# Sending x behind wq on the SP queue, and one V tile in two parts instead of four, in a decode kernel that streams its KV cache

## The chip, the core and the metric

One core of a Trainium2 chip runs the whole program. The metric is the device time in microseconds (us).

In the views, PE is TensorE (PEld its weight loads), DVE is VectorE, ACT is ScalarE, and SP is the engine that issues most transfers; a q behind a name means its sequencer. A semaphore is a counter that a transfer raises when its data have landed, and for which an engine can wait. A packet is the piece of a transfer that one of the 16 DMA engines moves at a time.

## The reference, cut to what matters

```python
# x [4,1,512], k_cache and v_cache [4,32,8192,128] bf16, wq [512,4096], wo [4096,512]; FFN width 1792
xn = layernorm(x)
q = (xn @ wq) per head
o = softmax(q . k_cache / sqrt(128)) @ v_cache
out = x + o @ wo + (silu(xn @ w_gate) * (xn @ w_up)) @ w_down
```

The K and V caches are 537 MB of the 551 MB that must be read. They come as 32 K tiles and 32 V tiles of 8 MB (4 heads each, 64 KB a partition).

## The kernel before: the parts concerned

Three 8 MB slots are used in turn. wq takes the first, and x, the layernorm's scratch and the q projection's scratch lie beside it; K0 and K1 take the other two. The first V tile can be loaded only when everything beside wq is finished.

```python
x_sb = beside_wq(B, D)                                   # 4 rows of 1 KB
nc.scalar.dma_start(out=x_sb, in_=x_flat[:, :])          # ACT's queue
nc.sync.dma_start(out=wq_t[:, 0:EC * H * Dh], in_=...)   # SP's queue, 4 MB
load_k(0); load_k(1)
# ... layernorm, transposition, q projection, zq ...
build_q(0); load_v(0)
for i in range(NT - 1):                                  # NT = 32
    turn_k(i, ...)                                       # VectorE transposes K_i
    if i >= 3:
        pv_to(i - 2, NK); load_k(i + 1)                  # K tile into the slot of V_(i-2)
    for g in range(NTG): score(i, g)                     # 64 matmuls
    ...
    elif i == NT - 2: load_v(i, (T // 4,) * 4)           # V30 in 4 transfers, T = 256
    else: load_v(i)                                      # one transfer of 8 MB
    # ... softmax of tile i, P.V of tile i-1 ...
# tail: wo, V31 in 7 parts of falling size, scores of K31, P.V of V30 and V31, wo, result
nc.sync.dma_start(out=out_flat[:, 0:DH], in_=res[0:B, :])
nc.scalar.dma_start(out=out_flat[:, DH:D], in_=res[QB:QB + B, :])
```

## Time and profile before

| | before |
|---|---|
| time, first three runs | 1286.03 us (1285.93 to 1286.06) |
| bytes, mean rate | 551.49 MB, 429 GB/s |
| DMA share, 0 to 1220 us / 1272 to 1279.4 us | 1.00 / 0.51 |
| last V part written | 1279.38 us |
| span in the profile | 1284.13 us |

The views that carry this (busy tenths, windows, end of the chain, timeline of the start) are shown in the prediction.

### The profile page before, as it was taken

To read this page: it belongs to the slowest core of one execution; us is meant where nothing else is said; L and a number is where in the kernel's file an instruction comes from. 1 tells how busy PE (TensorE), PEld (TensorE's weight loads), DVE (VectorE), ACT (ScalarE), POOL (GpSimd) and SP (SyncE) were. 2 spreads that over 40 slices of the span, in tenths; PEclk is the share of its full clock that TensorE was granted. 3 is DMA by queue.
4 is the path that set the end of the run, shared out by engine and by line. 5 is a ranking of instruction groups with operands and counts; after the bars stand their busy time and mean duration, and the time that the engine had idled before them with its cause. 6 is when DMAs were issued, how large, how long until landed. Compare 5 with 4: busy or idle time off the path is not lost.

```text
span 1284.1 us, 11309 instructions
## 1 busy us (share of the span) xinstructions
PE 1003.1 (78%) x5170; PEld 460.9 (36%) x5170; DVE 736.5 (57%) x621; ACT 30.1 (2%) x71; POOL 5.9 (0%) x12
## 2 busy tenths in 40 slices
PE   1697777977778977778877878877779787789785
PEld 0254333432334433333333333333334333334345
DVE  4846644665545665554665644666445766446651
ACT  1000000000000000000000000000000000000000
POOL 1000000000000000000000000000000000000000
PEclk8797889988899988889888899888899888899896
DMA  9999999999999999999999999999999999999997
GB/s 425 423 432 430 443 429 431 432 437 427 438 437 431 433 431 441 427 425 448 431 425 444 434 423 439 439 425 433 439 431 429 435 433 438 429 433 442 427 414 313
DMA packets 12600, 551.49 MB, mean 429 GB/s; under 512 B 1277, under 2 KB 1801, under 8 KB 3081
## 3 DMA queue, kind: packets, MB, share of 16 engines
q1 hardware_dynamic: 12536, 550.77, 99.2%
q8 instruction: 40, 0.66, 0.2%
q14 instruction: 8, 0.06, 0.0%
q10 hardware_dynamic: 16, 0.01, 0.0%
HBM read 550.77 MB, written 0.00 MB: 429 GB/s over the span
## 4 chain that ended last, share of the span: by engine, by line
DMA 53%; PE 35%; DVE 9%; SPq 2%; issue 0%; ACT 0%; DVEq 0%; ACTq 0%
DMA slot<-in_A_k_cache_dram 48%; PE sps L74 18%; PE oacc L74 16%; DVE slot L298 8%; DMA slot<-in_A_v_cache_dram 5%; SPq L117 1%; SPq L275 1%; PE mps L74 1%; DVE ptz L335 1%; PE yo_ps L74 0%; PE mps L317 0%; PE xps L74 0%; DVE oacc L368 0%; DVE o L370 0%; ACT p__1242 L326 0%
## 5 line engine op out<-in xcount | busy, mean ns | idle before, releaser
L298 DVE STREAM_TRANSPOSE slot<-slot 128x2048 uint32<-128x2048 uint32 (+1 forms) x198 | 561.8, 2901 | 294.7 <-DMA slot<-in_A_k_cache_dram 294.7
L74 PE MATMUL sps<-slot,zq 128*128 128x512 bf16 x2048 | 516.0, 415 | 246.5 <-DVE slot L298 246.4
L74 PE MATMUL oacc<-slot,ptz 128*16 128x512 bf16 x1920 | 430.8, 380 | 0.4 <-DMA slot<-in_A_v_cache_dram 0.4
L74 PEld LDWEIGHTS <-zq 128*128 128x128 bf16 x2048 | 210.9, 103 | 548.3 <-issue 226.2
L74 PEld LDWEIGHTS <-ptz 128*16 128x16 bf16 x1920 | 195.1, 106 | 209.4 <-issue 13.1
L311 DVE TENSOR_REDUCE mx<-sps 128x1 f32<-128x512 f32 x32 | 22.1, 692 | 97.1 <-PE sps L74 97.1
L74 PEld LDWEIGHTS <-slot 128*128 128x128 bf16 (+2 forms) x716 | 25.7, 110 | 20.6 <-DMA slot<-in_A_v_cache_dram 7.8
L345 DVE RECIPROCAL rcp<-mps 128x4 f32<-128x4 f32 x32 | 5.8, 183 | 46.2 <-PE mps L74 46.2
L320 DVE TENSOR_REDUCE nm<-mps 128x4 f32<-128x64 f32 x32 | 7.2, 225 | 36.1 <-PE mps L317 36.1
L74 PE MATMUL xps<-ptz,slot 128*128 128x4 bf16 x512 | 15.3, 169 | 7.3 <-DMA slot<-in_A_v_cache_dram 7.2
L74 PEld LDWEIGHTS mps<-rowb,rs 128*128 128x128 f32 x64 | 9.5, 187 | 14.3 <-issue 12.4
L74 PE MATMUL mps<-rowb,rs 128*128 128x4 f32 x64 | 12.3, 263 | 1.5 <-ACT p__323 L326 1.5
L74 PE MATMUL xps<-rowy,o 128*32 128x4 f32 (+1 forms) x226 | 10.7, 205 | 2.2 <-DVE o L370 2.2
L288 DVE COPY zq<-qt 32x8 bf16<-32x8 bf16 x64 | 11.1, 174 | 0.7
L74 PEld LDWEIGHTS xps<-rowy,o 128*32 128x32 f32 (+1 forms) x226 | 10.0, 155 | 2.8 <-DVE o L370 2.8
L317 PE MATMUL mps<-ident_f,mx 128*128 128x128 f32 x32 | 10.3, 322 | 0.8 <-DVE mx L311 0.8
L74 PE MATMUL yo_ps<-slot 128*4 128x128 bf16 (+1 forms) x60 | 3.6, 308 | 8.4 <-DVE yo_ps L167 6.8
L74 PE MATMUL yo_ps<-slot,otn 128*4 128x128 bf16 x128 | 6.4, 288 | 3.7 <-DMA slot<-in_A_wo_dram 3.5
L317 PEld LDWEIGHTS mps<-ident_f,mx 128*128 128x128 f32 x32 | 4.3, 133 | 13.8 <-DVE zq L288 6.3
L390 DVE TENSOR_TENSOR otn<-xps,rcp 32x16 bf16<-32x16 f32 x28 | 4.8, 170 | 6.6 <-PE xps L74 4.5
L380 DVE TENSOR_TENSOR otn<-xps,rcp 128x16 bf16<-128x16 f32 x1 | 0.2, 175 | 14.0 <-PE xps L74 14.0
L74 PEld LDWEIGHTS <-otn 128*4 128x4 bf16 x128 | 6.0, 115 | 3.9 <-issue 3.5
(146 smaller groups left out, 187.1 us busy)
## 6 DMA issues: line engine op xcount, KB each, us to landing
slot<-in_A_v_cache_dram SPq DMA_DIRECT2D x6, 2048.0 KB, 30.0
slot<-in_A_wq_dram SPq DMA_DIRECT2D x1, 4096.0 KB
slot<-in_A_wo_dram SPq DMA_DIRECT2D x1, 3584.0 KB, 31.3
slot<-in_B_w_gate_dram SPq DMA_DIRECT2D x1, 1792.0 KB, 24.5
slot<-in_B_w_up_dram SPq DMA_DIRECT2D x1, 1792.0 KB, 28.3
slot<-in_B_w_down_dram SPq DMA_DIRECT2D x1, 1792.0 KB, 32.5
slot<-in_A_v_cache_dram SPq DMA_DIRECT2D x1, 1536.0 KB, 21.3
slot<-in_A_v_cache_dram SPq DMA_DIRECT2D x1, 1024.0 KB, 22.5
```

The lines of the kernel that those rows point to most:

```text
L74: nc.tensor.matmul(out_ap, lhsT=lhsT, rhs=rhs, start=start, stop=True, skip_group_check=True, **kw)
L117: nc.sync.dma_start(out=t_[:, base:base + w * Dh], in_=src[:, t0 * Dh:(t0 + w) * Dh])
L275: nc.sync.dma_start(out=t_[:, n * D:H * D].rearrange("p (h e) -> p h e", e=D), in_=A_wo[n * P:H * P, :].rearrange("(h p) e -> p h e", p=P))
L288: nc.vector.tensor_copy(out=zq[a * QB:(a + 1) * QB, :, :, XO + a * QB].rearrange("p b (j r) -> p r j b", r=2), in_=qt[a * QB:(a + 1) * QB, ...
L298: nc.vector.transpose(out=ap, in_=ap)
L311: nc.vector.reduce_max(out=mx[:], in_=s_ps[n][:], axis=AX.X)
L317: nc.tensor.matmul(mps[:, 0:P], lhsT=nmx.pop(n)[:, 0:1].to_broadcast([P, P]), rhs=ident_f[:, :], is_transpose=True, start=True, stop=True, ...
L320: nc.vector.tensor_reduce(out=nm[:], in_=by_row(mps[:, 0:P]), axis=AX.X, op=ALU.max, negate=True)
L335: nc.vector.transpose(out=t_[y * QB:(y + 1) * QB, :, y, :, :].rearrange("p s u x -> p s (u x)"), in_=p_[y * QB:(y + 1) * QB, :].rearrange( ...
L345: nc.vector.reciprocal(out=rcp[j][:, :, b], in_=mps[:, P:P + HT])
L380: nc.vector.tensor_tensor(out=otn[:, j * HT:(j + 1) * HT, :], in0=xps[:], in1=rcp.pop(j)[:], op=ALU.mult)
L390: nc.vector.tensor_tensor(out=otn[q0:q1, j * 4:j * 4 + 4, :], in0=xps[q0:q1], in1=r_[q0:q1, y, :].unsqueeze(1).to_broadcast([QB, 4, B]), o ...
```

## The change

The diff, whole but for its file header:

```diff
     x_sb = beside_wq(B, D)
-    nc.scalar.dma_start(out=x_sb, in_=x_flat[:, :])
     nc.sync.dma_start(out=wq_t[:, 0:EC * H * Dh], in_=A_wq.rearrange("(p c) n -> p (c n)", c=EC))
+
+    nc.sync.dma_start(out=x_sb[0:B - 1, :], in_=x_flat[0:B - 1, :])
+    nc.sync.dma_start(out=x_sb[B - 1:B, :].rearrange("b (k e) -> b k e", k=2),
+                      in_=x_flat[B - 1:B, :].rearrange("b (k e) -> b k e", k=2))
@@
         elif i == NT - 2:
-            load_v(i, (T // 4,) * 4)
+            load_v(i, (T // 2, T // 2))
```

Its intent, as far as the diff shows it: x behind wq on the SP queue, in two transfers spread over three and two DMA engines, and a V block in two equal parts. The block in the diff is that of V30, the last V tile but one.

## The prediction

> **What bounds the kernel now.** I read the page's part 2 first, because it says whether any engine is busy from end to end.
>
> ```profile
> PE   1697777977778977778877878877779787789785
> ...
> DVE  4846644665545665554665644666445766446651
> ...
> DMA  9999999999999999999999999999999999999997
> GB/s 425 423 432 430 443 429 431 432 437 427 438 437 431 433 431 441 427 425 448 431 425 444 434 423 439 439 425 433 439 431 429 435 433 438 429 433 442 427 414 313
> ```
>
> TensorE and VectorE have gaps in every slice; the DMA row is full in all slices but the last. The page counts 551.49 MB at a mean of 429 GB/s, and 551.49 MB / 429 GB/s = 1285.5 us: the span is the time to move the bytes. The chain of waits in part 4 (DMA 53%, PE 35%, DVE 9%) must not be read as "35% of the span could be won on PE": its PE and DVE pieces lie beside a full DMA row. So I looked next at where the DMA stops being full, with windows cut at the end.
>
> ```profile
> 0.00:1220.00 1220.00, 957.99 (x4426) 429.79 (x4427) 712.57 (x599) 29.11 (x68) 5.87 (x12) 0.89 1.00 433
> 1220.00:1272.00 52.00, 39.41 (x600) 26.10 (x598) 23.47 (x20) 0.78 (x2) 0.00 (x0) 0.85 1.00 419
> 1272.00:1279.40 7.40, 3.99 (x116) 3.73 (x117) 0.00 (x0) 0.00 (x0) 0.00 (x0) 0.50 0.51 212
> 1279.40:1284.10 4.70, 1.70 (x36) 1.23 (x32) 0.46 (x2) 0.26 (x1) 0.00 (x0) 0.50 0.00 1
> ```
>
> The last two columns are DMA share and GB/s. The share is 1.00 up to 1272 us and 0.51 for 7.4 us after it: half of the 16 DMA engines are finished while the others still work. The packet records say why. A 65,536-byte packet takes 2.418 us (27.1 GB/s an engine, 434 for 16), and every engine gets the same bytes; but 40 packets of 16 KB on the instruction queue (page, part 3: q8, 40 packets, 0.66 MB) of 0.88 to 0.97 us each lie on the same engines. Seven engines finish the last transfer by 1272.3 us, the rest between 1275.7 and 1279.4 us. The last of these, not the mean, sets the end. Behind it comes a fixed tail of 4.7 us, seen at the end of the chain:
>
> ```profile
> 1255.84 23.23 DMA slot<-in_A_v_cache_dram
> ...
> 1279.11 0.59 PE xps L74 x16
> ...
> 1280.15 0.18 DVE otn L380
> 1280.38 1.03 PE yo_ps L74 x16
> ```
>
> So a change can win only by fewer bytes or packets on the slowest DMA engines, an earlier first byte, or a shorter tail.
>
> **What the Trainium skill says.** (1) "DMA: Bandwidth & Descriptors", section "Why a DMA increments its semaphore by 16 and not by 1": the number of engines of a transfer is the largest divisor up to 16 of the slowest dimension that is not 1 on both sides. That explains the shapes here: four rows of x use 4 engines before; three rows use 3, and one row cut into two uses 2. The trace before agrees for x: four packets of 1,024 bytes on the scalar queue. (2) The same page, "Issuing engines are not separate DMA queues": transfers issued elsewhere run on the same 16 engines, so moving x from ACT to SP frees no bandwidth. The trace agrees: one row of DMA activity, and queue q10 carries 0.01 MB. (3) The same page, "Where 436 GB/s comes from", gives 435.2 GB/s as the ceiling; the window above shows 433, so the stream has no slack to recover. (4) "Runtime: NRT & Kernel Launch", section "Instruction fetch mechanics": instructions come in 16 KiB blocks over a DMA queue. The 40 packets agree; the change leaves the number of matmuls alone, so I expect 40 again.
>
> **The change part by part: x.** It removes one ACT issue and adds two SP issues behind wq. The start before:
>
> ```profile
> 0.73 0.56 ACTq L96 DMA_DIRECT2D slot<-in_A_x_dram  x1
> ...
> 0.74 0.40 SPq L97 DMA_DIRECT2D slot<-in_A_wq_dram  x1
> ...
> 1.20 0.89 SPq L104 DMA_DIRECT2D slot<-in_A_k_cache_dram  x2
> ...
> 6.81 0.40 DVE L179 CAST slot<-slot 4x512 f32<-4x512 bf16 x1
> ...
> 12.95 3.60 PE L74 MATMUL sps<-slot,xnt_w 128*32 128x512 bf16 x32 [1.56 <-DMA slot<-in_A_wq_dram]
> ...
> 19.50 0.33 SPq L117 DMA_DIRECT2D slot<-in_A_v_cache_dram  x1
> 20.11 0.74 DVE L288 COPY zq<-qt 32x8 bf16<-32x8 bf16 x4
> 32.25 13.28 DVE L298 STREAM_TRANSPOSE slot<-slot 128x2048 uint32<-128x2048 uint32 x6 [11.39 <-DMA slot<-in_A_k_cache_dram]
> ```
>
> Before, the layernorm (from the cast at 6.81 to the copy into xnt_w that ends at 11.68 us, 4.87 us) ran while wq was still coming. Afterwards x lands just behind wq, at an estimated 13.2 us (PE saw wq at 12.95), so the layernorm runs from 13.2 to 18.1 us and the q matmuls begin at about 18.2 instead of 12.95: this front slips by some 5.3 us. Everything behind it slips alike: the first V load goes out at about 24.8 us instead of 19.50, and the first zq copies end at about 26.1 instead of 20.85. What needs them is later still. VectorE waits 11.39 us for the first K tile, until 32.25 us, so about 6 us of slack remain. The DMA queue holds K0 and K1 to about 51 us, so a V load issued at 24.8 has 26 us to spare. On the path: nothing. The queue's own cost: a 1,024-byte packet of x took 0.044 us, with 0.009 us for its semaphore, at most twice on two engines and once on a third: under 0.15 us on those, and the scalar queue had put a packet on four engines before. I book 0.0 to +0.1 us. K0 and K1 are issued some 0.9 us later, under a wq that keeps the engines busy to 12 us: hidden.
>
> **The V tile.** The diff changes the last V tile but one (V30) from four parts of 2 MB to two of 4 MB. On the fastest engine the packet records give 19.319 us for a whole tile and four times 4.86 = 19.44 us for the quarters; halves should cost about 19.36 (an estimate: 8 packets more than a whole tile, not 24). That saves 0.08 us on every DMA engine, and this is on the path. The arrivals get coarser:
>
> ```profile
> 1230.71 17.66 DVE L298 STREAM_TRANSPOSE slot<-slot 128x2048 uint32<-128x2048 uint32 x8 [2.71 <-DMA slot<-in_A_k_cache_dram]
> ...
> 1241.40 0.98 PE L74 MATMUL xps<-ptz,slot 128*128 128x4 bf16 x32
> ...
> 1251.70 3.48 PE L74 MATMUL xps<-ptz,slot 128*128 128x4 bf16 x128
> ...
> 1258.82 5.34 PE L74 MATMUL yo_ps<-slot,otn 128*4 128x128 bf16 x112 [3.48 <-DMA slot<-in_A_wo_dram]
> ```
>
> K31 is seen at 1230.7; one half of V30 later (9.7 us) it is 1240.4, and PE wants it at 1241.40. The second half lands at about 1250.1, wanted at 1251.70. A slip of 1 us would still disappear in the 3.48 us that PE waits for wo.
>
> **The sum.** DMA stream -0.08 (V30) and 0.0 to +0.1 (x). One more term: the scalar queue's first DMA is now that of the result. Its first issue took 0.56 us before, the one at the end 0.28 us; if the difference is a first-use cost, up to +0.28 us moves into the tail. I take +0.1. Together 1286.03 - 0.08 + 0.05 + 0.1 = 1286.1, rounded toward no change: **1286.0 us**.
>
> **Rivals.** (A) The late x becomes the start's bound: the layernorm would delay the first scores or starve the queue. For it: the front slips by 5.3 us. Against it: 6 and 26 us of slack. If it came, up to 2 us. (B) The coarser V30 holds up PE, keeps K31's slot, and delays the last V loads. For it: about 1 us of slack only. Against it: the last part was issued at about 1259.1, 20 us before it landed. It would make no difference below some 10 us of slip. (C) A gain in the tail: SP stood 11.32 and 12.37 us in two issues there, and fewer packets queued should let it through earlier. Against it: all 16 engines stayed busy to 1272, so earlier issues win nothing. (D) The instruction fetches fall differently on the slow engines: up to 1 us either way at the last engine, the largest term of my range.
>
> **Range and chances.** The three runs before lie within 0.13 us. The terms of the sum span about 0.4 us and (D) adds some 0.5: 1285.3 to 1286.6. Two per cent is 25.7 us; even evening out all 16 engines would win only about 4 us, and no rival costs over 2 us. So within 2%: 0.99; faster 0.004; slower 0.006.
>
> **What would show it.** DMA share still 1.00 to about 1272 and near 0.5 after; 40 instruction packets; the q matmuls starting near 18 us and the first V issue near 25; the first transposition still at about 32.2; the last V part landing within 0.5 us of 1279.1; the ACT issue of the result longer than 0.28 us if first use costs. The prediction is wrong if the half-idle stretch at the end changes its length, or if the DMA row shows a hole before 60 us.

## More of the kernel before

Experiments were sent in four batches; each is compared with the runs of the kernel before of its own batch (a batch need not have met the same chip as another).

One more belongs here, as it became decisive: who SP waited for in the last microseconds (waiter, releaser, us in total, times, longest).

```profile
SPq L487 <- DVE res L485: 22.5, 1, 22.5
SPq L512 <- DMA out_dram<-res: 1.0, 1, 1.0
SPq L512 <- PEq L512: 0.6, 2, 0.4
```

The last matmul ends at 1281.4 us, the span at 1284.1. These lines say that some 1.6 us of the rest are SP waiting for the result to land and for the engines to meet.

## The result, and the profile after

| | before | after |
|---|---|---|
| median (range), 6 runs each | 1285.98 us (1285.83 to 1286.09) | 1285.60 us (1285.47 to 1285.66) |
| ratio, 95% interval | | 0.9997, 0.9984 to 1.001 |
| span in the profile | 1284.13 us | 1283.89 us |
| instruction packets (q8) | 40 | 40 |
| last V part written | 1279.379 us | 1279.383 us |

A ratio is the mean time of one kernel's runs over that of the other's runs of the same rounds, so it is not quite the ratio of the medians. By the interval the two are the same; the ranges do not overlap, though, and a repeat gave 0.34 us again (below). So there is a small gain of some 0.35 us to explain, where the prediction had 0.03.

The start of the changed kernel, as a timeline (start us, us, engine, line, operation, count, idle before and its releaser):

```profile
0.74 0.39 SPq L96 DMA_DIRECT2D slot<-in_A_wq_dram  x1
...
1.19 0.34 SPq L98 DMA_DIRECT2D slot<-in_A_x_dram  x1
...
1.57 0.24 SPq L99 DMA_DIRECT2D slot<-in_A_x_dram  x1
...
13.02 0.41 DVE L182 CAST slot<-slot 4x512 f32<-4x512 bf16 x1 [6.13 <-DMA slot<-in_A_x_dram]
...
17.95 3.61 PE L74 MATMUL sps<-slot,xnt_w 128*32 128x512 bf16 x32 [0.33 <-DVE xnt_w L204]
...
24.54 0.33 SPq L120 DMA_DIRECT2D slot<-in_A_v_cache_dram  x1
25.16 0.74 DVE L291 COPY zq<-qt 32x8 bf16<-32x8 bf16 x4
32.28 4.50 DVE L301 STREAM_TRANSPOSE slot<-slot 128x2048 uint32<-128x2048 uint32 x2 [6.38 <-DMA slot<-in_A_k_cache_dram]
```

The layernorm now waits for x, and everything behind it is 5.0 us later than before; VectorE is still ready 6.38 us before the first K tile is there. Nothing is lost. The windows of the end (the last two columns are DMA share and GB/s):

```profile
1220.00:1272.00 52.00, 40.35 (x599) 26.07 (x597) 23.47 (x20) 0.78 (x2) 0.00 (x0) 0.84 0.99 418
1272.00:1279.40 7.40, 3.98 (x116) 3.72 (x117) 0.00 (x0) 0.00 (x0) 0.00 (x0) 0.50 0.53 218
```

Half the DMA engines still idle for the last 7 us. The chain's end has the same last landing, 1279.07 us, and the same last block of matmuls at 1279.11 as before:

```profile
1255.92 23.15 DMA slot<-in_A_v_cache_dram
1279.07 0.05 issue
1279.11 0.59 PE xps L74 x16
...
1280.36 1.03 PE yo_ps L74 x16
```

The spans, however, differ by 0.245 us. So in this pair of profiles the difference lies behind the last matmul. (What larger V30 packets save is not seen at the last landing of this pair, because the stream of the changed kernel came to V30 0.36 us later, at 1223.12 instead of 1222.76 us; it is measured below.) There the timelines say, before and then after:

```profile
1281.72 0.35 SPq L487 DMA_DIRECT2D out_dram<-res  x1
1281.72 0.28 ACTq L488 DMA_DIRECT2D out_dram<-res  x1
```

```profile
1281.70 0.29 SPq L490 DMA_DIRECT2D out_dram<-res  x1
1281.71 0.62 ACTq L491 DMA_DIRECT2D out_dram<-res  x1
```

and SP's waits after, against 1.0 us before:

```profile
SPq L515 <- DMA out_dram<-res: 0.7, 1, 0.7
```

The instruction records of SP explain it. This is not a view of the page but the raw records (start in us, time taken in us, semaphores waited for; "result" marks the one that a half of the result's transfer raises):

```
before                                            after
1281.718  0.348  issue of SP's half               1281.702  0.288  issue of SP's half
1282.123  0.028  S106, S105                       1282.042  0.028  S104, S103
1282.187  0.972  S107, S102 (SP's result)         1282.107  0.028  S107, S102
1283.193  0.028  S108, S100 (ACT's result)        1282.168  0.732  S108, S101 (SP's result)
1283.258  0.028  S109, S101                       1282.937  0.028  S109, S100
1283.319  0.028  S110, S104                       1283.074  0.028  S110 (ACT's result), S106
1283.384  0.007  first drain                      1283.139  0.007  first drain
```

At the end SP waits for every transfer semaphore, in five instructions of two semaphores each. Eight semaphores are given to the transfers in turn (ACT's half of the result is counted just before SP's); so **the number of transfers in the kernel decides which of the five waits the result's two semaphores fall into**. An already satisfied wait costs 0.061 to 0.065 us from one to the next. Before, three such waits stood behind the one that blocked; after, ACT's half is in the last of the five. The change has one transfer fewer in all (one more for x, two fewer for V30), and so moves the turn by one. From the issue of SP's half to its first drain it is 1.666 us before and 1.437 after: 0.229 us. From that drain to the end of the span it is 0.748 us in both.

### The profile page after: what moved, and what is told of

Same layout as the page of the kernel before. It is cut to its first block, busy times and chain, and to the rows that moved or that the text cites. A ratio compares the mean times of both kernels' runs of the same rounds, so it can differ in the third digit from the quotient of the medians.

```text
span 1283.9 us, 11309 instructions
## 1 busy us (share of the span) xinstructions
PE 1008.6 (79%) x5170; PEld 462.0 (36%) x5170; DVE 736.6 (57%) x621; ACT 30.2 (2%) x71; POOL 5.9 (0%) x12
## 4 chain that ended last, share of the span: by engine, by line
DMA 55%; PE 36%; DVE 9%; SPq 0%; issue 0%; ACT 0%; DVEq 0%; ACTq 0%
DMA slot<-in_A_k_cache_dram 50%; PE sps L74 19%; PE oacc L74 15%; DVE slot L301 8%; DMA slot<-in_A_v_cache_dram 5%; PE xps L74 0%; DVE ptz L338 0%; PE mps L74 0%; PE mps L320 0%; SPq L120 0%; PE yo_ps L74 0%; ACT p__5209 L329 0%; ACT p__324 L329 0%; DVE oacc L371 0%; DVE mx L314 0%
## 5 line engine op out<-in xcount | busy, mean ns | idle before, releaser
L74 PE MATMUL sps<-slot,zq 128*128 128x512 bf16 x2048 | 521.4, 418 | 237.7 <-DVE slot L301 237.6
L74 PE MATMUL mps<-xnt_w,slot 128*128 128x4 bf16 x112 | 6.8, 199 | 0.3 <-DVE rcp L348 0.3
```

The lines of the kernel that those rows point to most:

```text
L74: nc.tensor.matmul(out_ap, lhsT=lhsT, rhs=rhs, start=start, stop=True, skip_group_check=True, **kw)
```

## The experiments

**Theory** (closing waits): the gain is mostly where the result's semaphores fall, the rest is fewer V30 packets. **Rivals**: it is the V30 packets alone (stream); it is x off the ACT queue at the start (start). Four kernels separate the parts.

**lanes_only**: the kernel before, with V30 in three parts; the number of transfers becomes that of the changed kernel.

```diff
-            load_v(i, (T // 4,) * 4)
+            load_v(i, (T // 2, T // 4, T // 4))
```

> The kernel before (x on ACT) with V30 in three parts (128, 64, 64 columns) instead of four: one transfer fewer, so the completion semaphores (eight, taken in turn) of the result's two transfers become those of the changed kernel (SP's the third, ACT's the fifth of SP's five closing waits, instead of second and third), with x as before. Closing-wait theory: about 1285.7, most of the 0.4 us gain, with the ACT issue at the end still short (0.28 us). Stream theory (the gain is the larger V30 packets): a third to a half of 0.08 us, 1285.95. Start theory (the gain is x off the ACT queue): no gain, 1286.0.

**v_only**: the second half of the diff alone.

> The V30 half of the change alone (two parts), x on ACT as before: two transfers fewer, so the result's semaphores come last in SP's closing waits (ACT's fourth, SP's fifth). Closing-wait theory: 1285.6 or a little less, the ACT issue at the end short. Stream theory: 1285.9. Start theory: 1286.0.

**x_only**: the first half of the diff alone.

> The x half of the change alone, V30 in four parts: one transfer more than before, so the result's semaphores are waited for first and second of five (SP's in the first). Closing-wait theory: not faster than before, 1286.0 to 1286.2 (four waits of 0.065 us behind the last landing instead of three, ACT issue at the end 0.6 us). Start theory: all of the gain, 1285.6. Stream theory: 1286.0.

**x_one**: the changed kernel with x in one transfer.

```diff
-    nc.sync.dma_start(out=x_sb[0:B - 1, :], ...)
-    nc.sync.dma_start(out=x_sb[B - 1:B, :]..., ...)
+    nc.sync.dma_start(out=x_sb, in_=x_flat[:, :])
```

> The changed kernel with x in one transfer of four rows on SP instead of two: one transfer fewer, result's semaphores last (ACT fourth, SP fifth of five). Closing-wait theory: 0.05 to 0.1 us under the changed kernel, 1285.5. If the split of x into two (three and one engines) has a worth of its own in the stream: slower than the changed kernel, 1285.7 or more.

A fifth kernel, **act_warm**, was run last, to settle the term of the prediction on the ACT queue's first use: only the fourth row of x goes from ACT, which keeps count and semaphores of the changed kernel.

```diff
-    nc.sync.dma_start(out=x_sb[B - 1:B, :].rearrange(...
+    nc.scalar.dma_start(out=x_sb[B - 1:B, :].rearrange(...
```

> The changed kernel with only the fourth row of x sent from ACT instead of SP: same number of transfers, same semaphores for the result (SP third, ACT fifth of the closing waits), same V30, but the ACT queue has issued one transfer before the result's. Theory that a first use delays the result (my prediction's term): ACT's last issue 0.28 us instead of 0.62, the result lands earlier, 0.1 to 0.2 us under the changed kernel. Rival, from the profiles so far (last landing 1.44 us behind the issue where ACT had been used, 1.39 where not): SP's half of the result lands last, 1.44 us after its issue, with two closing waits behind it, so from that issue to SP's first drain 1.60 us as in lanes_only, not 1.44: some 0.15 us over the changed kernel, 1285.75.

And the changed kernel once more, as **after_again**:

> The changed kernel once more, on the chip of the two runs beside it, as their measure: 0.2 to 0.4 us under the kernel before, 1285.6. No theory differs here.

Measured, five runs each (before and after: six). "Waits" are the numbers, of SP's five closing waits, that hold SP's and ACT's half of the result. "Issue to drain" is from the issue of SP's half to SP's first drain. "Stretch" is the time, on the DMA engine that is first, from the end of K31 to the first packet of the second wo transfer; it holds V30 and the first wo transfer, and nothing else changes in it.

| kernel | V30 parts | waits SP, ACT | issue to drain | stretch | median | minus before of its batch |
|---|---|---|---|---|---|---|
| before | 4 | 2, 3 | 1.666 us | 28.148 us | 1285.98 us | |
| lanes_only | 3 | 3, 5 | 1.603 | 28.105 | 1285.77 | -0.09 us |
| v_only | 2 | 5, 4 | 1.511 | 28.061 | 1285.66 | -0.20 |
| x_only | 4 | 1, 2 | 1.612 | 28.149 | 1285.89 | +0.03 |
| x_one | 2 | 5, 4 | 1.509 | 28.062 | 1285.62 | -0.24 |
| act_warm | 2 | 3, 5 | 1.507 | 28.061 | 1285.77 | -0.20 |
| after | 2 | 3, 5 | 1.437 | 28.061 | 1285.60 | -0.38 |
| after_again | 2 | 3, 5 | 1.440 | 28.061 | 1285.58 | -0.34 |

Two columns explain the last one. The stretch gives 0.0435 us for each part of V30 (28.148, 28.105, 28.061). Adding the differences of both columns to the kernel before gives, for lanes_only, v_only, x_only, x_one, act_warm and after: -0.11, -0.24, -0.05, -0.24, -0.25 and -0.32 us. Measured were -0.09, -0.20, +0.03, -0.24, -0.20 and -0.38. All agree within 0.09 us, about what the medians can resolve.

- The **start theory falls**: x_only, which has all of it, gains nothing (+0.03).
- The **stream theory** is right about its term but too small: 2 x 0.0435 = 0.087 us.
- The **closing waits** carry the rest. lanes_only differs from before only in the places of the two halves and in one part of V30: the wait that blocks is the third of five instead of the second, and its issue-to-drain is 0.063 us shorter, one wait. All eight profiled kernels with the changed kernel's places and no earlier ACT transfer (after, after_again and the six below) have 1.437 to 1.450 us from issue to drain.
- The two parts of the diff **do not add up**: v_only -0.20 and x_only +0.03 make -0.17, both together -0.38. Each moves the turn of the semaphores, by -2 and +1, and what matters is where the sum comes to rest. The odd second transfer of x does no work that one transfer does not do as well (x_one: -0.24 against -0.34 to -0.38); a plausible reason for it is this count, but the diff does not say so.
- On the ACT queue: in before, lanes_only, v_only and act_warm, where ACT had issued a transfer earlier, its last issue took 0.28 us; in the others, where it was the first, 0.60 to 0.62. Yet the last landing, read from the last blocked wait, came 1.44 us behind SP's issue in the former and 1.37 to 1.39 in the latter. **With a cold ACT queue (one that had issued nothing) the last landing came 0.06 to 0.07 us earlier, not later.** act_warm came in at 1285.77 as its rival said, but by another way: SP's half landed after 1.27 us, not 1.44, and ACT's was the last. So the sign of the effect is shown; why the slower issue lands the pair earlier is not. The packet records narrow it down: the last packet of the pair ends 0.946 us after SP's issue in before and in act_warm and 0.955 us after it in the changed kernel, so the gain arises between that packet and the semaphore's last step (0.47 to 0.48 us against 0.40).

**How much room the front has.** The prediction held that the late x is hidden by 6 us (VectorE) and 26 us (queue). x_after_k0 and x_after_k1 move the two x transfers of the changed kernel behind the first and the second K tile.

```diff
     load_k(0)
+    (the two x transfers)          # x_after_k1: one line lower
     load_k(1)
```

> Changed kernel with the two x transfers behind the first K tile instead of behind wq: x lands near 32 us, the layernorm and the q projection run from 32 to about 44 us, the first V load is issued near 44 us and the first scores start near 46 instead of 34.6. Slack theory (the front is hidden while the queue holds K1 to 51 us): no change, 1285.6. If the front is on the path: the first scores are 11 us late and the end with them, 1297.

> The same behind the second K tile: x lands near 51 us, the first V load can be issued only near 63 us, while the DMA queue runs dry at 51. Slack theory: the DMA row shows a hole of about 12 us and the end is 10 to 13 us later, 1296 to 1299. If even this is hidden: 1285.6.

Measured: 1294.78 us (+8.85 over its before) and 1314.12 (+28.19). The first lies between my two alternatives, the second is twice the forecast. x_after_k0's windows (DMA share and GB/s last) and the issue of the K2 load in its timeline:

```profile
60.00:83.00 23.00, 15.28 (x61) 6.26 (x60) 19.51 (x17) 0.78 (x2) 0.00 (x0) 0.85 0.98 419
83.00:91.50 8.50, 7.76 (x35) 3.15 (x33) 6.49 (x7) 0.00 (x0) 0.00 (x0) 1.00 0.16 55
...
90.39 0.33 SPq L104 DMA_DIRECT2D slot<-in_A_k_cache_dram  x1
```

and the same issue in the changed kernel:

```profile
77.31 0.33 SPq L107 DMA_DIRECT2D slot<-in_A_k_cache_dram  x1
```

The first V load was indeed in time (43.97 us, no hole at 51). The hole comes later: the DMA engines run empty between 83.0 and 84.7 us and start again at 91.4. The first transposition started 13.07 us late (45.35 against 32.28), and the load of K2, which waits for the work on tiles 0 and 1, is 13.08 us late as well: that work took up none of the delay. Of the 13.08 us the queue hid 4 to 5 (the time grew by 8.85). So the real room behind the change is 6.4 us in VectorE plus 4 to 5 us at K2, not 26. My 26 us looked at the next load alone, not at the one after. x_after_k1 costs twice the forecast because it has both holes: 51 to 64 us before the first V load (issued at 63.38), and about 100 to 111 us before K2 (issued at 109.80).

**V30 coarser and finer.** v30_whole loads V30 in one part (V29 in two, to keep the count); v30_ten in ten parts.

```diff
-        elif i == NT - 2:                          # v30_whole
+        elif i == NT - 3:
             load_v(i, (T // 2, T // 2))
```

```diff
-            load_v(i, (T // 2, T // 2))            # v30_ten
+            load_v(i, (32,) * 6 + (16,) * 4)
```

> Changed kernel with V30 as one transfer (and V29 in two halves, to keep the number of transfers and so the semaphores). PE gets V30 only near 1250 us instead of 1240, the last scores slip by some 9 us and K31's slot comes free near 1262 instead of 1253. Stream theory: 1285.5 to 1285.6, as the queue still holds V31's first half to 1265 to 1270. Rival B of the prediction (the slot is freed too late): up to 2 us more, 1286 to 1288.

> Changed kernel with V30 in ten parts (six of 1 MB, four of 512 KB), eight transfers more, which brings the eight semaphores round to the same place. By the packet records 8,192 bytes take 0.309 us and 4,096 bytes 0.159 us (with 0.015 us for each semaphore), against 2.418 for 65,536: the tile costs 48 x 0.309 + 32 x 0.159 + 0.15 = 20.07 us instead of 19.36, so the end is 0.7 us later: 1286.3. If packet size is not on the path: 1285.6.

Measured: v30_ten 1285.85 us, 0.28 above the changed kernel (taken as 0.36 under before). Its stretch is 28.410 us: eight parts more cost 0.349, again 0.0435 each. My 0.7 was wrong, because I had added the durations of packets; packets overlap a little, and the difference between starts is what counts. v30_whole is 1287.55 us, though its stretch is the shortest of all (28.018) and its last V part is written at 1279.1, no later. PE's waits from 1225 us on:

```profile
PE xps L74 <- DMA slot<-in_A_v_cache_dram: 7.6, 1, 7.6
PE sps L74 <- DVE slot L301: 6.1, 1, 6.1
PE xps L74 <- issue: 3.2, 2, 2.0
```

PE stands 7.6 us for V30, and all its later work moves against the end. There it stops three more times in its dense run of small matmuls, for 0.42, 2.04 and 1.17 us (until 1268.75, 1274.67 and 1279.77), without waiting for a semaphore ("issue"), and reaches the last one 1.6 us late. The trace suggests what these stops are: they lie exactly 256 PE records (matmuls and weight loads) apart, and each ends 1.25 to 1.35 us after an instruction fetch (queue q8) ended. So PE seems to have run out of instructions there; no experiment tested this. So rival B exists, but one step further off than the change went. In the changed kernel PE came to V30 at 1242.85 us instead of 1241.40; PE's waits show none for V30 there, and the granted clock was lower (0.66 against 0.83 from 1230 to 1240 us), which is the likely reason; it cost nothing, as PE still waited 1.84 us for wo.

**Do the instruction fetches set the end?** more_pe adds 33 tiny matmuls to each of 31 tiles, into a spare corner of PSUM.

```diff
         nc.vector.reciprocal(out=rcp[j][:, :, b], in_=mps[:, P:P + HT])
+        if n < NT - 1:
+            for _ in range(33):
+                mm(mps[0:B, 256:256 + B], xnt_w[:, 0, 0:B], xnt_w[:, 0, 0:B], start=True)
```

> The changed kernel with 33 tiny matmuls (4 columns) more in each of 31 tiles, into a spare corner of PSUM: 1,023 matmuls with their weight loads, 2,046 instructions or eight 16 KB fetches more (48 instead of 40), about one for each DMA engine that carries fetches. They take some 2 us of PE in each 39 us tile, where PE has 8 us or so to spare. Theory that the engines carrying fetches set the end: each fetch put its engine back by about 1.45 us, so the end is 1.4 us later, 1287.0, and the half-idle stretch at the end grows from 7.4 to 8.9 us. If PE's time were on the path: up to 60 us later. If neither: 1285.6.

Measured: 1287.03 us, 1.45 above after_again in the same batch. Page line and window of more_pe:

```profile
q8 instruction: 48, 0.79, 0.2%
...
1272.00:1280.70 8.70, 5.07 (x158) 4.72 (x155) 0.00 (x0) 0.00 (x0) 0.00 (x0) 0.50 0.52 216
```

The last V part was written at 1280.65 us against 1279.14 in after_again. The packet records of that part show 16 engines. Seven ended early in both (1272.2 to 1272.6 us against 1271.6 to 1272.4). One was a little later and did not move (1276.3 in both). Eight moved with the fetches: one from 1277.8 to 1279.2, seven from 1278.7 to 1279.1 to 1280.3 to 1280.6. The durations of the fetches repeat with a period of eight, so these eight seem to take them in turn, five each in the changed kernel. The data were the same, PE still waited for V31 at the end, and eight fetches more cost 1.45 us. So the half-idle stretch is the fetches' doing on eight engines (an estimate: 5 x 1.45 = 7.3 us; they end about 7 us behind the first seven). What holds the one engine at 1276.3 is open.

**A version to use the idle engines** failed. engine0 has one DMA engine alone load the first 4 of V30's 256 columns (127 rows in one transfer, one row in another), x in one transfer and V31's first half in one.

```diff
...
+            for p0, p1 in ((0, P - 1), (P - 1, P)):
+                nc.sync.dma_start(out=t_[p0:p1, 0:4 * Dh], in_=src[p0:p1, 0:4 * Dh])
+            v_from(i, t_, 4 * Dh, 4, (T // 2 - 4, T // 2))
...
```

> Changed kernel with x in one transfer, V31's first half in one, and the first 4 of V30's 256 columns loaded by one engine alone (127 rows, then 1 row), 128 KB taken off the other engines' shares. Packet tracking after the x transfer suggests that the first engine carries no fetches and ends 7 us early; 128 packets of 0.046 us cost it 5.9 us, while each other engine is relieved of 8 KB, 0.30 us, less 0.04 us for one more transfer. If the slowest engines set the end and the first one is idle at the end: 0.2 to 0.3 us under the changed kernel. If the first engine carries fetches: about 5 us later than the changed kernel.

Measured: 1289.00 us, with an unusual spread (1288.25 to 1293.39); the profile is that of the slowest run, 1293.39. Its timeline and a window of V30:

```profile
1212.89 10.55 SPq L434 DMA_DIRECT2D slot<-in_A_v_cache_dram  x1
...
1240.00:1250.00 10.00, 10.00 (x131) 5.83 (x130) 9.61 (x5) 0.00 (x0) 0.00 (x0) 1.00 0.99 353
```

With 127 rows queued on one engine, SP's next issue stood for 10.55 us, so the rest of V30 was issued at 1223.5 us, when the first engines were already empty. After this the stream ran at 353 to 359 GB/s through V30 instead of 433 (32,768-byte packets of 1.40 us in the median instead of 1.21), with all engines busy. The cause of the low rate is open. The run tells nothing on whether the first engine carries fetches.

The changed kernel itself stays the fastest that was run; x_one is some 0.1 us behind it.

## Why the prediction was right or wrong

The time, 1285.60 us, lies in the range of 1285.3 to 1286.6, and the class (within 2%) is right. By its own steps:

- **The bound.** Right: the DMA row stays full to 1272 us and half empty after it, with 40 fetches, and more_pe shows the fetches' price at the end. Two readings on the way were loose. Bytes over mean rate give the span by definition, so only the full DMA row carries the argument. And 1272.3 and 1275.7 us are not ends of whole engines: these are 1272.5 and 1276.2.
- **x at the start.** Right to 0.3 us: x used at 13.02 (13.2 told), q matmuls at 17.95 (18.2), V load at 24.54 (24.8), zq done at 25.90 (26.1), 6.38 us of slack left. The cost booked for it, 0.0 to 0.1 us, fits x_only: +0.03, or +0.08 when its end, 0.05 us shorter, is taken off. The 26 us of room in the queue was wrong, as x_after_k0 shows: 4 to 5, at K2. It did not matter here.
- **The shape of x.** Wrong in a detail: one row written as two pieces was recorded as one row of 1,024 bytes, so x came on three engines and one, not three and two (four packets of 1,024 bytes each before and after; the second transfer's semaphore rose by a single step when the data landed).
- **V30.** Right: -0.08 us told, -0.087 measured in the stream.
- **The ACT queue's first use.** The lengthening of the issue came (0.62 against 0.28 us), but the step from it to +0.1 us in the tail failed: the last landing came 0.06 to 0.07 us earlier.
- **"A fixed tail of 4.7 us".** This is the step that cost most. From the last V packet to the end of the span it is 4.75 us before and 4.50 after. The closing waits, which the change reorders without touching them, gave 0.16 us (0.225 to 0.065 us from the last landing to the first drain).
- **The sum.** The terms added up to +0.07 us, and -0.03 was told, by rounding toward no change; measured were -0.38 (repeat -0.34). So the sign of the sum was wrong. That the result still lies in the range is partly luck: the range owes its width to term D, which did not come. Replacing the failed terms: -0.087 (V30) -0.069 (last landing) -0.160 (waits behind it) = -0.32 us.
- **Rivals.** A did not come, but its size was badly told: the first step beyond the room costs 9 us, not 2. B did not come; v30_whole shows it at some 2 us over the changed kernel (1.62 over before) for PE being held up 7.6 us, below the 10 us that I called harmless. C was right that nothing would come of SP's long issues: one shortened (11.32 to 6.14 us, the second wo transfer), the other grew (12.37 to 16.15 us). D, my largest term, did not come: 40 fetches in both, and the last V part within 0.004 us in the two profiles (that of after_again was 0.24 us earlier, so single profiles do vary by this much).

## What to carry to other kernels

When two kernels differ by a few tenths of a microsecond, read the last instructions behind the last matmul: the program's own closing waits are part of the time, and a transfer more or less anywhere moves which of them blocks. Where a stream sets the end, look at each DMA engine's end and not at the mean; instruction fetches rode on some of them here, so matmuls that were hidden on PE were not free. And when telling how late something may come, follow the delay to every later issue that depends on it, not only to the next one.

## What the Trainium skill lacked or had wrong

- "Runtime: NRT & Kernel Launch", section "Instruction fetch mechanics", calls the cost of a 16 KiB boundary mostly hidden. In the changed kernel no wait of PE's at the end is down to it, but each fetch holds a data DMA engine: eight more fetches made the end 1.45 us later (more_pe). In v30_whole PE seems to have stood for fetches as well, 0.42 to 2.04 us at a time. No page says that the fetches fall on some of the 16 engines only (eight here, by the packet records).
- No page tells of the closing waits: five waits on SP, 0.061 to 0.065 us from one to the next, in an order that the number of transfers shifts against the result's semaphores (1.437 to 1.666 us from the result's issue to the drain).
- "DMA: Bandwidth & Descriptors", section "Why a DMA increments its semaphore by 16 and not by 1", derives the engines from the slowest dimension as the instruction carries it. It does not say when a cut row is carried whole: one written as 2 x 256 elements moved as one packet of 1,024 bytes on one engine.
- No page has the difference between a first and a later issue on ACT (0.53 to 0.62 against 0.28 us), nor that the result landed 0.06 to 0.07 us earlier with the slow one.
- No page gives the depth at which an issue stands still: behind 127 rows on one engine SP's next issue took 10.55 us (engine0). The drop from 433 to 353 GB/s that followed, with all engines busy, is not explained by any run here.
